# Taking turns between two streams of matmuls: a turn at every half group of products in place of every whole one

## The chip, the cores and the metric

The kernel runs on one core of one Trainium2 chip. The metric is the device time of one execution in microseconds (us). The engines are named as in the profile: PE is TensorE's matrix multiply and PEld its loading of weights, DVE is VectorE, ACT is ScalarE, POOL is GpSimd, SP is SyncE, which issues most of the DMAs. PSUM is the accumulator memory that PE writes; ACT and DVE copy ("evacuate") it to SBUF. Each engine works through its own instructions in one fixed order.

## The reference, cut to what matters

Forward and backward pass of two branches that share a normalised input: an S4 layer (a long convolution by FFT, with gradients for its parameters) and a gated feed-forward network. Sizes: 2048 rows, model width 576, hidden width 4608, 128 states. The result is the output and the gradients of the input and of eleven parameter arrays.

```python
def _A_ref(u, A_re, ..., Dskip):                       # S4
    K = jnp.einsum("dn,dnl,dn->dl", Cc, P, dB).real      # 576 kernels of length 2048
    Yf = rfft2(up) * rfft2(Kp)
    y = irfft2(Yf)[..., :L] + u * Dskip
def _B_ref(x, W_gate, W_up, W_down):                   # FFN
    gate = x @ W_gate; up = x @ W_up
    h = gate * (gate > 0) * up
    return h @ W_down
def f(...): xn = layernorm(A_u); return A_u + _A_ref(xn, ...) + _B_ref(xn, ...)
out, vjp = jax.vjp(f, ...); return out, *vjp(grad_out)
```

## The kernel before

Two Python generators write the program. `Ffn.gen` issues the feed-forward work, `S4.gen` the convolution work, and each hands control back with `yield us`, where `us` is its own figure for the work it has just issued. The loop at the end of the main function drives them: it takes one step of the FFN and adds its `us`; then it takes steps of S4 until S4's sum has caught up with `PACE` = 0.9 of the FFN's. S4 starts only when all four groups of the layer norm are done. So the places of the `yield`s in the FFN are the only places where S4's instructions can be issued, and the figures beside them say how much of S4 is issued there. Tile, the layer below, keeps this order as a priority when it puts each engine's instructions in a row: an instruction whose inputs it takes to be late can be passed by a later one.

The FFN runs over 12 chunks of 384 hidden columns (`FTC` = 3 blocks of 128) and 4 groups of 512 rows. For each chunk there are these pieces:

- `a_unit` (L228 on): three products of five matmuls (`NK` = 5, 128x512, L244): gate, up, and the gradient of h. Each has one PSUM bank of the pool `ps_mm`, which has three. When all three are issued, ACT makes `rg` (L252), DVE makes `upm` (L254), `hT` (L256), `dgT` (L262) and `duT` (L264), and one copy makes `dhb`. Before the `yield` of each product, `t_steps` (L273) issues four transposes per step into one of two `pt` banks, and a copy to `hN`, `dgN` or `duN`.
- `outdx` (L278 on): for one block of 128 rows, four products of 288 columns (L300): two of three matmuls for the output (`which` = 0) and two of six for the gradient of the input (`which` = 1). Each is copied to `osx`, and POOL issues a DMA that adds `osx` to `acc_dram` (L313).
- `dw_down` (L338): three groups of 16 matmuls of 144 columns in one bank. `dw_gu` (L354): two products of 16 matmuls of 384 columns. `dw_left` (L372): the same for the last 64 columns of width.

S4 works through PSUM banks of its own, `ps_s4`, of which there are three. `fwd1` (L627) transforms the long way; `mix` (L644) does the 16-point transform in two matmuls with 64 weight columns each, which write the upper and the lower half of one bank; `product` multiplies on DVE; `unmix` (L654) transforms back; `back2` (L684) ends it. `p2` makes the kernels and their gradients: long DVE and ACT steps (L838 to L876), then in `turn` and `sums` eight small matmuls (L901), eight transposes (L911) and eight matmuls (L925) a time, one bank each. Nearly every S4 bank is emptied by one copy (L68 on ACT or L62 on DVE, chosen by `Balance`, which keeps two running sums) and then used by a later S4 step.

For the last chunk the FFN yields the word "last" before the closing pieces: then all that is left of S4 is issued, and `Final` joins both branches (L1048 to L1093).

Of the kernel before, what the change touches and what calls it, by code (L numbers as in the profile page):

```python
# [21 lines left out]
ST = 16  # L22
DH = D // 2
NK = 5
DP = NK * P
Fc = 384
FTC = Fc // P
# [133 lines left out]
class Ffn:  # L161
# [68 lines left out]
    def a_unit(self, c, sg, ft, turns=()):  # L230

        g, nc = self.g, self.g.nc
        src = self.t_steps(turns)
        xT, gT = self.X[(c, sg)]
        fs = slice(ft * P, (ft + 1) * P)
        pss = []
        dhb = self.dh0.get(ft) if (c, sg) == (0, 0) else None
        for i, rhs in enumerate((xT, xT, gT)):
            if i == 2 and dhb is not None:
                continue  # L240
            w = self.wd[i]
            ps = g.psum_mm.tile([P, 512], F32, name="ps_mm")
            for k in range(NK):
                nc.tensor.matmul(ps[:], lhsT=w[:, k, fs], rhs=rhs[:, k, :], start=(k == 0), stop=(k == NK - 1))  # L244
            pss.append(ps)
            for _ in turns:
                next(src)
            yield NK * 0.2158 + len(turns) * 0.22
        ps_g, ps_u = pss[0:2]
        shp = [P, JS * P]  # L250
        rg = self.ep.tile(shp, BF16, name="rg")
        nc.scalar.activation(rg[:], ps_g[:], ACT.Relu)  # L252
        upm = self.ep.tile(shp, BF16, name="upm")
        nc.vector.scalar_tensor_tensor(upm[:], rg[:], 0.0, ps_u[:], op0=ALU.is_gt, op1=ALU.mult)  # L254
        hT = self.tp.tile(shp, BF16, name="hT")
        nc.vector.tensor_tensor(hT[:], rg[:], upm[:], op=ALU.mult)  # L256
        g.bal.add(d=1.6, a=0.48)
        if dhb is None:
            dhb = self.ep.tile(shp, BF16, name="dhb")[:]
            g.bal.copy(dhb, pss[2][:], 512)  # L260
        dgT = self.tp.tile(shp, BF16, name="dgT")
        nc.vector.tensor_tensor(dgT[:], dhb, upm[:], op=ALU.mult)  # L262
        duT = self.tp.tile(shp, BF16, name="duT")
        nc.vector.tensor_tensor(duT[:], dhb, rg[:], op=ALU.mult)  # L264
        self.T[(c, sg, ft)] = (hT, dgT, duT)
# [11 lines left out]
    def outdx(self, c, sg, j, last=None, turns=()):  # L277

        g, nc = self.g, self.g.nc
        t = sg * JS + j  # L280
        js = slice(j * P, (j + 1) * P)
        if last is None:
            o = self.op.tile([P, 2, D], BF16, name="osx")
        else:
            last.begin(t)
        src = self.t_steps(turns)
        Ts = [self.T[(c, sg, ft)] for ft in range(FTC)]
        for which in range(2):
            for hf in range(2):
                hs = slice(hf * DH, (hf + 1) * DH)  # L290
                if which == 0:
                    mms = [(Ts[ft][0], self.wf[:, 0, ft, hs]) for ft in range(FTC)]
                else:
                    mms = [(Ts[ft][1], self.wf[:, 1, ft, hs]) for ft in range(FTC)] + [(Ts[ft][2], self.wf[:, 2, ft, hs]) for ft in range(FTC)]
                mms = [(lt[:, js], rh) for lt, rh in mms]
                if last is not None:
                    mms = last.terms(t, which, hf) + mms
                ps = g.psum_mm.tile([P, 512], F32, name="ps_mm")
                for i, (lt, rh) in enumerate(mms):
                    nc.tensor.matmul(ps[:, :DH], lhsT=lt, rhs=rh, start=(i == 0), stop=(i == len(mms) - 1))  # L300
                if last is None:
                    g.bal.copy(o[:, which, hs], ps[:, :DH], DH)
                else:
                    last.take(t, which, hs, ps[:, :DH])
                next(src, None)
            if which == 0:
                yield FTC * 0.245
        if last is not None:
            last.end(t)
        elif c == 0:  # L310
            nc.gpsimd.dma_start(g.acc_dram[:, t, :, :], o[:])
        else:
            nc.gpsimd.dma_start(g.acc_dram[:, t, :, :], o[:], accum_op=ALU.add)  # L313
        yield FTC * 0.49

    def rows(self, c, i):

# [11 lines left out]
    def dw_down(self, c, q):  # L329
        g, nc = self.g, self.g.nc  # L330
        f0 = c * Fc
        gq = self.rows(c, q)
        if q % 2 == 0:
            self.obd = self.rp.tile([P, FTC, DH], BF16, name="obd")
        ps = g.psum_mm.tile([P, 512], F32, name="ps_mm")
        for ft in range(FTC):
            for st in range(ST):
                nc.tensor.matmul(ps[:, ft * 144:(ft + 1) * 144], lhsT=self.hN[:, st, ft * P:(ft + 1) * P], rhs=gq[:, st, :], start=(st == 0), stop=(st == ST - 1))  # L338
            if ft < FTC - 1:
                yield ST * 0.0625  # L340
        g.bal.copy(self.obd[:, :, (q % 2) * 144:(q % 2 + 1) * 144], ps[:, 0:FTC * 144].rearrange("p (f c) -> p f c", c=144), FTC * 144)
        if q % 2 == 1:
            hs = slice((q // 2) * DH, (q // 2 + 1) * DH)
            nc.sync.dma_start(self.dWd[f0:f0 + Fc, hs].rearrange("(t p) d -> p t d", p=P), self.obd[:])
        yield ST * 0.0625

    def dw_gu(self, c, k):
        g, nc = self.g, self.g.nc
        f0 = c * Fc
        xs = self.rows(c, 4 + k)  # L350
        for src, dst in ((self.dgN, self.dWg), (self.duN, self.dWu)):
            ps = g.psum_mm.tile([P, 512], F32, name="ps_mm")
            for st in range(ST):
                nc.tensor.matmul(ps[:, :Fc], lhsT=xs[:, st, 0:P], rhs=src[:, st, :], start=(st == 0), stop=(st == ST - 1))  # L354
                if st == ST // 2 - 1:
                    yield ST * 0.0813
            ob = self.rp.tile([P, Fc], BF16, name="obw")
            g.bal.copy(ob[:], ps[:, :Fc], Fc)
            nc.sync.dma_start(dst[k * P:(k + 1) * P, f0:f0 + Fc], ob[:])
            yield ST * 0.0813  # L360

    def dw_left(self, c):

# [870 lines left out]
```

## Time and profile before

| what | value |
| --- | --- |
| three runs, median (lowest to highest) | 1853.74 us (1851.06 to 1854.6) |
| the profiled execution, its own time | 1854.6 us |
| its span, first to last instruction | 1852.9 us |
| mean granted clock of TensorE | 0.989 |
| PE busy, instructions | 1744.4 us, 16257 |
| DVE busy, ACT busy | 1379.2 us, 1173.9 us |
| first and last S4 matmul start | 73.3 us, 1616.4 us |

How to read it: "busy" is the time in which an engine has an instruction under way, and matmuls overlap, so that a matmul of 288 columns that counts 288 ns follows the one before it after only 122 ns. An engine's "idle before" is named with what ended it. Lines such as L68 are those of a helper that many callers share; the tile that is written tells which caller it was. "issue" stands for idle time that no other instruction is seen to end.

### The profile page before, as it was taken

The page shows a single profiled execution, that of the slowest core. Times are in us where ns is not written, and L with a number is a line of the kernel's source. Part 1 is how long each engine was busy: PE and PEld are TensorE (multiplying, and loading weights), DVE is VectorE, ACT ScalarE, POOL GpSimd, SP SyncE. Part 2 cuts the span into 40 slices and gives each one's busy share as a digit, 9 for nine tenths or more (in the row PEclk, how much of TensorE's full clock was granted, in tenths as well). Part 3 has the DMA queues.
Part 4 walks back from the last instruction along what each step waited for, and adds up shares of the span by engine and source line. Part 5 has one row for each costly group of instructions (what it writes and reads, how often), then busy time and mean ns, then how long its engine had stood idle before and what let it go on. Part 6 is the DMA issues. An engine that isn't in the chain of part 4 may idle for free. (4 is left out here: it accounts for less than half of the span.)

```text
span 1852.9 us, 41883 instructions
## 1 busy us (share of the span) xinstructions
PE 1744.4 (94%) x16257; PEld 1182.4 (64%) x16257; DVE 1379.2 (74%) x3223; ACT 1173.9 (63%) x2647; POOL 206.5 (11%) x246
## 2 busy tenths in 40 slices
PE   7989989999999999999999999999999998899888
PEld 5655547667566666766766766766766764476556
DVE  7565875686798787787887889889878657924772
ACT  5865855686587488477487567657748746732432
POOL 0200002012012012002102101102201100010000
PEclk9989999999999999999999999999999999999999
DMA  8798988678567666776776856856754779785763
GB/s 287 264 323 292 328 237 261 195 182 220 182 129 192 191 184 166 211 187 139 207 202 136 233 156 154 236 159 122 195 174 97 183 240 269 203 216 179 232 195 102
DMA packets 236411, 373.26 MB, mean 201 GB/s; under 512 B 49202, under 2 KB 153140, under 8 KB 234676
## 3 DMA queue, kind: packets, MB, share of 16 engines
q1 hardware_dynamic: 210244, 304.08, 50.8%
q0 software_dynamic: 24384, 51.92, 18.8%
q10 hardware_dynamic: 1584, 14.60, 2.3%
q8 instruction: 127, 2.08, 0.4%
q14 instruction: 72, 0.59, 0.1%
HBM read 233.08 MB, written 137.43 MB: 200 GB/s over the span
## 5 line engine op out<-in xcount | busy, mean ns | idle before, releaser
L68 ACT CAST osx<-ps_mm 128x288 bf16<-128x288 f32 x684 | 261.7, 422 | 73.8 <-PE ps_mm L300 62.2
L313 POOL DMA_DIRECT2D acc_dram<-osx x160 | 139.8, 877 | 1038.1 <-ACT osx L68 581.0
L300 PE MATMUL ps_mm<-wf,dgT 128*128 128x288 bf16 x1152 | 209.1, 288 | 17.8 <-ACT osx L68 12.4
L354 PEld LDWEIGHTS <-rows 128*128 128x128 bf16 x1536 | 145.9, 98 | 95.9 <-issue 3.0
L300 PE MATMUL ps_mm<-wf,duT 128*128 128x288 bf16 x1152 | 207.1, 288 | 0.0
L300 PE MATMUL ps_mm<-wf,hT 128*128 128x288 bf16 x1152 | 186.4, 288 | 8.5 <-ACT osx L68 2.6
L244 PE MATMUL ps_mm<-xT,wd_158 128*128 128x512 bf16 x720 | 182.5, 379 | 0.7 <-ACT xT L153 0.7
L244 PE MATMUL ps_mm<-gT,wd_160 128*128 128x512 bf16 x705 | 181.4, 383 | 0.7 <-ACT obw L68 0.7
L244 PE MATMUL ps_mm<-xT,wd_159 128*128 128x512 bf16 x720 | 180.6, 379 | 0.0
L254 DVE SCALAR_TENSOR_TENSOR upm<-rg,ps_mm 128x512 bf16<-128x512 bf16 x144 | 98.3, 683 | 99.6 <-PE ps_mm L244 82.8
L338 PE MATMUL ps_mm<-rows,hN 128*128 128x144 bf16 x2304 | 158.2, 228 | 0.0
L338 PEld LDWEIGHTS <-hN 128*128 128x128 bf16 x2304 | 149.1, 99 | 8.1 <-issue 5.6
L300 PEld LDWEIGHTS <-dgT 128*128 128x128 bf16 x1152 | 109.7, 98 | 54.1 <-issue 25.8
L354 PE MATMUL ps_mm<-duN,rows 128*128 128x384 bf16 x768 | 138.6, 326 | 0.0
L354 PE MATMUL ps_mm<-dgN,rows 128*128 128x384 bf16 x768 | 136.6, 326 | 0.0
L300 PEld LDWEIGHTS <-hT 128*128 128x128 bf16 x1152 | 107.7, 98 | 42.7 <-issue 13.1
L300 PEld LDWEIGHTS <-duT 128*128 128x128 bf16 x1152 | 113.1, 98 | 32.0 <-issue 2.4
L68 ACT CAST obw<-ps_mm 128x384 bf16<-128x384 f32 x105 | 50.2, 478 | 125.8 <-PE ps_mm L354 89.6
L68 ACT CAST dhb<-ps_mm 128x512 bf16<-128x512 f32 x141 | 83.9, 595 | 66.3 <-PE ps_mm L244 64.6
L930 DVE TENSOR_REDUCE Sm<-pr 128x8 f32<-128x256 f32 x288 | 119.5, 415 | 3.6
L252 ACT ACTIVATE rg<-ps_mm 128x512 bf16<-128x512 f32 x144 | 86.9, 603 | 54.4 <-PE ps_mm L244 52.9
L244 PEld LDWEIGHTS <-wd_159 128*128 128x128 bf16 x720 | 65.4, 98 | 61.4 <-issue 1.2
(2513 smaller groups left out, 3516.2 us busy)
## 6 DMA issues: line engine op xcount, KB each, us to landing
acc_dram<-osx POOLq DMA_DIRECT2D x176, 288.0 KB, 4.8
gT<-in_gT_dram SPq DMA_DIRECT2D x48, 640.0 KB, 6.3
xT<-xT_dram SPq DMA_DIRECT2D x44, 640.0 KB, 6.2
rows<-in_gq_dram SPq DMA_DIRECT2D x48, 576.0 KB, 4.5
wf<-in_Wf_dram ACTq DMA_DIRECT2D x11, 1296.0 KB, 8.8
ex_dram<-exs SPq DMA_DIRECT2D x18, 640.0 KB, 5.6
ex<-ex_dram SPq DMA_DIRECT2D x36, 320.0 KB, 3.4
out_dram<-obw SPq DMA_DIRECT2D x96, 96.0 KB, 2.7
```

What stands on the lines that cost most here:

```text
L68: self.nc.scalar.copy(out, in_)
L244: nc.tensor.matmul(ps[:], lhsT=w[:, k, fs], rhs=rhs[:, k, :], start=(k == 0), stop=(k == NK - 1))
L252: nc.scalar.activation(rg[:], ps_g[:], ACT.Relu)
L254: nc.vector.scalar_tensor_tensor(upm[:], rg[:], 0.0, ps_u[:], op0=ALU.is_gt, op1=ALU.mult)
L300: nc.tensor.matmul(ps[:, :DH], lhsT=lt, rhs=rh, start=(i == 0), stop=(i == len(mms) - 1))
L313: nc.gpsimd.dma_start(g.acc_dram[:, t, :, :], o[:], accum_op=ALU.add)
L338: nc.tensor.matmul(ps[:, ft * 144:(ft + 1) * 144], lhsT=self.hN[:, st, ft * P:(ft + 1) * P], rhs=gq[:, st, :], start=(st == 0), stop=(st = ...
L354: nc.tensor.matmul(ps[:, :Fc], lhsT=xs[:, st, 0:P], rhs=src[:, st, :], start=(st == 0), stop=(st == ST - 1))
L930: nc.vector.tensor_reduce(out=Sm[:, vi, s0 + dd:s0 + dd + DG, :], in_=pr[:], op=ALU.add, axis=AX.X)
```

## The change

Five `yield`s of the FFN are split, so that control goes to S4 at about every half product; the figures are split with them, and their sum for a piece of work stays the same (in `outdx` 6 x 3 x 0.1225 instead of 3 x 0.245 + 3 x 0.49; with the closing terms of the last chunk two more are yielded). No instruction is added or taken away, and no buffer.

```diff
@@ a_unit: after two of the five matmuls, and after the product
             for k in range(NK):
                 nc.tensor.matmul(ps[:], lhsT=w[:, k, fs], rhs=rhs[:, k, :], ...)
+                if k == 1:
+                    yield 2 * 0.2158
             pss.append(ps)
             for _ in turns:
                 next(src)
-            yield NK * 0.2158 + len(turns) * 0.22
+            yield (NK - 2) * 0.2158 + len(turns) * 0.22
@@ outdx: at every three matmuls
                 for i, (lt, rh) in enumerate(mms):
                     nc.tensor.matmul(ps[:, :DH], lhsT=lt, rhs=rh, ...)
+                    if len(mms) - i == FTC + 1:
+                        yield FTC * 0.1225
                 if last is None:
                     g.bal.copy(o[:, which, hs], ps[:, :DH], DH)
...
-            if which == 0:
-                yield FTC * 0.245
+                if which + hf < 2:
+                    yield FTC * 0.1225
...
-        yield FTC * 0.49
+        yield FTC * 0.1225
@@ dw_down: at every 8 of 16 matmuls
                 nc.tensor.matmul(ps[:, ft * 144:(ft + 1) * 144], ...)
+                if st == ST // 2 - 1:
+                    yield ST * 0.03125
             if ft < FTC - 1:
-                yield ST * 0.0625
+                yield ST * 0.03125
...
-        yield ST * 0.0625
+        yield ST * 0.03125
@@ dw_gu: at every 4 of 16 matmuls
                 nc.tensor.matmul(ps[:, :Fc], lhsT=xs[:, st, 0:P], ...)
-                if st == ST // 2 - 1:
-                    yield ST * 0.0813
+                if st % 4 == 3 and st < ST - 1:
+                    yield 4 * 0.1625
             ob = self.rp.tile([P, Fc], BF16, name="obw")
             g.bal.copy(ob[:], ps[:, :Fc], Fc)
             nc.sync.dma_start(dst[k * P:(k + 1) * P, f0:f0 + Fc], ob[:])
-            yield ST * 0.0813
+            yield 4 * 0.1625
```

## The prediction

> **What bounds the kernel now.** First the page's busy times, then the stages, then PE's waits.
>
> ```profile
> span 1852.9 us, 41883 instructions
> ...
> PE 1744.4 (94%) x16257; PEld 1182.4 (64%) x16257; DVE 1379.2 (74%) x3223; ACT 1173.9 (63%) x2647; POOL 206.5 (11%) x246
> ```
>
> PE is the bound: 108.5 us of the span are all that it idles. The change adds no instruction, so it can only move that idle time, and the shorter delays that the overlap of matmuls hides in "busy". The stages (time, PE, PEld, DVE, ACT, POOL, clock, DMA share, GB/s) say where it lies:
>
> ```profile
> 0.00:73.00 73.00, 60.58 (x490) 41.05 (x491) 46.30 (x159) 46.24 (x99) 9.99 (x30) 1.00 0.86 285
> 73.00:295.00 222.00, 201.04 (x1488) 125.28 (x1486) 158.86 (x363) 151.00 (x336) 18.71 (x31) 0.94 0.88 285
> 295.00:902.00 607.00, 592.14 (x6070) 413.51 (x6067) 463.13 (x1015) 415.91 (x945) 87.84 (x91) 1.00 0.72 190
> 902.00:1502.00 600.00, 578.05 (x5800) 398.52 (x5798) 513.67 (x1175) 402.26 (x896) 76.08 (x78) 1.00 0.67 171
> 1502.00:1617.00 115.00, 98.99 (x658) 55.05 (x658) 83.10 (x264) 75.57 (x206) 6.92 (x8) 0.99 0.87 246
> ```
>
> Idle PE: 12.4 us before S4 starts at 73, then 21.0, 14.9, 22.0 and 16.0, and 22.4 after S4 has ended. Only the four stages with S4 in them, 73.8 us together, can answer to where S4's turns stand. In the last of them PE waits for the inverse transforms' writes (a copy into `fC` that waits for a DMA), and in the built order of the changed kernel all but one of the last 19 of its 32 `fC` tiles have as much PE work between their matmuls as before: I leave that stage out.
>
> Whom PE waits for, largest first:
>
> ```profile
> PE ps_mm L300 <- ACT osx L68: 15.0, 24, 2.4
> PE pt L273 <- DVE dgT L262: 11.5, 7, 4.0
> ...
> PE ps_s_2084 L627 <- ACT fA_2074 L68: 3.6, 1, 3.6
> PE pt L273 <- ACT hN L68: 3.3, 3, 2.9
> PE ps_mm L300 <- DVE osx L62: 2.9, 1, 2.9
> PE ps_s_1667 L627 <- DVE fA_1626 L62: 2.9, 1, 2.9
> ```
>
> Nothing large repeats; PE waits for copies out of banks, FFN's and S4's alike, a little at a time. So I also added up, over all starts of matmuls from 73 to 1617 us, the time by which each came later than the one before it allows when packed (122 ns after one of 288 columns, 216 after 512, 162 after 384, 62 after 144, 55 after 128, 25 after L901 and L925). This catches what "busy" hides. At the first matmul of a bank, with the price of a mode change (below) taken off, the delays come to 124 us: 69.4 at S4's banks, 34.1 at L300's, 15.8 at L273's, 4 at the rest.
>
> **The change, part by part.** Counted in the two built orders of PE, where a "turn" is S4 work between two FFN matmuls:
>
> *More and shorter turns.* S4's 1046 banks stand in 622 turns before and in 781 after; 424 are second or later in their turn before, 265 after (six in a row falls from four times to once). The delays before are 49.9 us at the 622 first ones (0.080 each) and 19.5 at the 424 later ones (0.046 each). A later one waits because the copy of a neighbour, 0.40 to 0.42 us on ACT for 288 columns, has not freed a bank. What moves out of a burst gets at least a quarter product in front of it: 0.37 us of L300, 0.43 of L244, 0.5 of L338, 0.65 of L354. I take it that these 159 lose their 0.046 us, **-7.3 us**, and that the delay at first ones, whose inputs come from DVE steps and DMAs at their own times, stays 49.9 in sum. Bounds: -19.5, if all later delays go, and +5.4, if each new first costs what the firsts cost (159 x (0.080 - 0.046)).
>
> *More mode changes.* `mix` uses 64 weight columns, and PE pays to go there and back:
>
> ```profile
> 181.23 0.60 PE L244 MATMUL ps_mm<-xT,wd_158 128*128 128x512 bf16 x2
> 181.77 0.31 PE L644 MATMUL ps_s_2640<-b_ug,FM 128*64 128x288 bf16 x2
> 182.01 0.82 PE L244 MATMUL ps_mm<-xT,wd_158 128*128 128x512 bf16 x3
> ```
>
> The second L244 starts at 181.459 (in the trace's rows), the pair follows 0.309 later where 0.216 is packed (0.093 lost), the next L244 after 0.246 where 0.122 is packed, and where another pair follows instead it starts after 0.147, so 0.1 is lost on leaving and 0.01 more in the spacing after it: 0.20 in all. Entries into `mix` from anything else are 143 before and 157 after: 14 x 0.20 = **+2.8 us**. Bounds: 0, where PE would have waited there anyway, and +2.8.
> The Trainium skill speaks against the change here: "TensorEngine Tiling (Array Packing)", Key Properties, says that a change of tiling mode drains TensorE. An estimate from "TensorE: Matmul & The Clock Gate", Single matmul latency, which gives about 166 ns beyond the streaming at full clock, would put two drains at 0.33 us and the 14 at +4.6, which would make the sum below -2.7; the row has less, and I use the row.
>
> *FFN banks.* A turn inside a product holds its `ps_mm` bank longer, and that product's copy is now issued behind the turn's copies. I measured in the orders how much PE work lies between the end of a product and the start of the one that takes its bank: for the 640 starts of L300 the mean stays, the starts with under 0.9 us in the commonest pairing rise from 36 to 51. By the trace a start with 0.6 to 0.8 us in between lost 0.083 us, one with 0.8 to 1 us 0.045, one with 1 to 1.2 us 0.100: no slope, so the price is **0**, with +1.5 (15 x 0.1) as the upper bound and -1.5 as the lower. The three banks of `a_unit` are freed only by L252 and L254 after the third product, before and after. The cover of L273's two `pt` banks changes as little (11 of 362 starts below 1.2 us, before and after).
>
> *What else moves with a turn.* S4's DMAs on SP (`A_ug`, `C_dk`, `ex`, `dkr`, `Kst`) and its long DVE and ACT steps are issued at most half a product (0.4 to 0.65 us) sooner or later, against 3 to 6 us to landing; SP passes no transfer over more than a turn, POOL's `acc_dram` adds keep their order, `Balance` moves seven copies between ACT and DVE (0.40 against 0.46 us). I price it at 0; the work that hides it is the FFN product under way. If that cover goes, what is late is `upm` (L254) behind a DVE step of 0.8 to 1.5 us, and then L244's banks: the wait is in the profile already, and a bound of +-4 us is one more or less of the longest DVE-made wait in the list above, 4.0.
>
> Sum: -7.3 + 2.8 + 0 + 0 = **-4.5 us** against the profiled execution's own 1854.6 (the span and 1.7 around it), hence 1850.1; that execution was 0.9 above the median of 1853.74, and against the median it is **1849.2**. Best bounds: -19.5 - 1.5 - 4 = -25; worst: +5.4 + 2.8 + 1.5 + 4 = +13.7.
>
> **The rivals.**
>
> *No change that can be told.* Within 0.2%, 3.7 us, one measurement of this kernel can't tell a change from none (three runs of one program lie 3.5 us apart). Priced by the cover of each S4 bank instead of its place in the turn, the delays go from 69.4 only to 67.5: covers under 0.6 us fall from 30 to 9, but those between 0.6 and 1 rise from 74 to 90. Then -1.9 + 2.8 = +0.9, **1854.6**. For it: Tile already puts S4 into products (50 of 99 turns within L244 products stand inside one). Against it: the delays of later ones in a turn are real rows.
>
> *A new wait at every new turn (slower).* PE runs in order; each of 159 new turns is one more place where it meets an S4 matmul whose input, made by DVE (`pr_z`, `pr`, `Y`; DVE is 86% busy from 902 to 1502), isn't there. At the firsts' 0.080: +5.4 + 2.8 = +8.2, **1862**. It decides from 0.052 us per new turn on (159 x 0.052 - 7.3 + 2.8 = 3.8). For it: 49.9 of the 69.4 us lie at firsts. Against: a later start also gives DVE more time.
>
> *The clock as well (much faster).* After the stall at 102 us PE ran at half speed:
>
> ```profile
> 102.00:107.00 5.00, 2.01 (x14) 1.06 (x13) 5.00 (x6) 4.54 (x6) 0.00 (x0) 0.90 0.96 337
> 107.00:112.00 5.00, 3.93 (x17) 1.85 (x17) 4.23 (x9) 3.77 (x9) 0.00 (x0) 0.50 1.01 392
> 112.00:118.00 6.00, 6.00 (x39) 4.41 (x38) 3.64 (x9) 2.41 (x7) 0.54 (x1) 0.65 0.98 322
> ```
>
> If the even turns of `fwd1` avoid that stall (2.9) and the slow clock after it (5 x 0.10 + 5 x 0.50 + 6 x 0.35 = 5.1), the sum is -4.5 - 2.9 - 5.1 = -12.5: **1841**. Against it: DVE is full there with three `exs` steps (L584), which stand together in the new order too.
>
> **How the numbers follow.** The forecast (faster, -4 to -8) has 0.34, the rival of the clock 0.08, no change 0.26, slower 0.32. So faster 0.42, same 0.26, slower 0.32; the predicted time is 1849.2. The range runs from 1838 to 1866: from the clock rival's time and 3 more down to the new waits' time and 4 more, inside the bounds on the good side (1829) and to just short of +13.7 (1867.4) on the other. The forecast's own range is 1845 to 1851.
>
> **What would show it.** Right: entries to L644 at 157 with the same 0.1 us lost on each side; fewer waits of L627, L654 and L911 on copies; idle PE from 73 to 1502 down from 57.8 by some 4; 1617 to the end unchanged at 236 us. The forecast is wrong if the idle time before S4's matmuls grows with the number of turns, or if L300's wait on `osx` (15.0) grows by more than 2 us. A half-speed stretch more or less (3.4 us of it cost 1.7) would blur all of this.

## The result, and the profile after

| | kernel before | changed kernel |
| --- | --- | --- |
| median (lowest to highest) of 4 runs each | 1854.17 us (1851.06 to 1855.16) | 1866.77 us (1864.97 to 1870.59) |
| profiled execution, its own time | 1854.6 us | 1865.62 us |

The ratio is 1.0074, with a 95% interval of 1.0053 to 1.0094: slower by 12.6 us, where -4.5 was forecast, and 0.8 us outside the range. These four runs of one kernel lie 4 to 6 us apart, so the sign is not in doubt; what it says of the change is another matter, to which the experiments come.

The page's busy times of the changed kernel:

```profile
span 1863.9 us, 41883 instructions
...
PE 1747.0 (94%) x16257; PEld 1180.6 (63%) x16257; DVE 1386.5 (74%) x3222; ACT 1176.7 (63%) x2648; POOL 206.9 (11%) x246
```

The same number of instructions, the same share of PE. DVE alone is busier by a sum that needs a reason, 7.3 us with one instruction less: its instructions have become longer. The stages, cut at the same events as before (start of S4, first L907, and so on; columns as before):

```profile
0.00:73.00 73.00, 60.07 (x491) 40.51 (x491) 46.30 (x159) 46.39 (x100) 9.99 (x30) 1.00 0.85 285
73.00:304.00 231.00, 205.03 (x1562) 128.44 (x1560) 160.47 (x362) 155.99 (x348) 27.49 (x38) 0.96 0.92 293
304.00:907.00 603.00, 586.84 (x5996) 406.25 (x5992) 466.69 (x1013) 411.41 (x933) 80.35 (x84) 1.00 0.69 183
907.00:1514.00 607.00, 578.82 (x5802) 399.18 (x5801) 515.92 (x1178) 403.87 (x897) 75.20 (x78) 0.99 0.66 170
1514.00:1628.00 114.00, 100.74 (x654) 55.80 (x653) 82.17 (x262) 75.45 (x204) 6.92 (x8) 0.97 0.88 246
```

Idle PE in the four stages with S4: 26.0, 16.2, 28.2 and 13.3 us, 83.6 together against 73.8 before. In the first three of them it is 70.4 instead of 57.8, where the prediction named some 4 us less as a sign of being right. What follows the last S4 matmul is unchanged (236.1 us against 236.5). The second stage has lengthened by 9 us and holds 74 matmuls more, the third is 4 shorter and holds 74 fewer; the fourth is 7 longer. By the ends of the FFN's chunks in the two traces, the changed kernel is 3 us ahead after the first chunk, 1 behind after the third and 13 behind after the eighth, and then stays at 11 to 13 (last matmul of `dw_gu` in each chunk). It is no single event, though it has one that stands out. The waits of PE, total us, times, longest:

```profile
PE ps_mm L302 <- ACT osx L68: 17.8, 17, 6.4
...
PE pt L275 <- DVE dgT L264: 9.1, 7, 3.6
PE ps_mm L302 <- DVE upm L256: 8.5, 10, 3.0
```

and of the kernel before, beside the 15.0 for `osx` that the prediction shows:

```profile
PE ps_mm L300 <- DVE upm L254: 2.0, 5, 0.8
```

(Lines have moved down: L300 is now L302, L273 L275, L254 L256, L252 L254, L627 L633, L644 L650, L313 L317, L354 L360, L828 and L829 L834 and L835.) The first line is the one that the prediction named as its test: fewer waits, but a larger sum, and one of 6.4 us. The waits for `upm` have grown by more, 6.5 us, 3.0 of it in one wait at 107 us, in a stall that PE has in both kernels. From 73 us to the last S4 matmul, waits of over 1 us number 31 and sum to 58.5 us; before, 26 and 48.2. These 10.3 us are nearly as much as the 11.0 by which the profiled executions differ.

The chain of that wait, in the timeline of the changed kernel (start, length, engine, line, operation; in brackets the idle time before it and what ended it):

```profile
285.14 1.20 POOL L834 COPY dkc<-dkr 128x512 bf16<-128x512 bf16 x1 [7.59 <-issue]
...
285.47 1.22 DVE L845 TENSOR_SCALAR W<-xa 128x640 f32<-128x640 f32 x1
...
286.32 1.73 POOL L835 TENSOR_TENSOR dkc<-dkr,lv 128x512 bf16<-128x512 bf16 x1
...
286.73 2.00 DVE L846 SCALAR_TENSOR_TENSOR W<-W,xa 128x640 f32<-128x640 f32 x1
...
288.00 1.64 POOL L834 COPY dkc<-dkr 128x512 bf16<-128x512 bf16 x1
...
288.76 0.74 ACT L847 ACTIVATE W<-W 128x640 f32<-128x640 f32 x1 [2.10 <-DVE W L846]
...
289.58 0.87 POOL L317 DMA_DIRECT2D acc_dram<-osx  x1
...
289.84 0.90 PE L302 MATMUL ps_mm<-wf,hT 128*128 128x288 bf16 x6 [1.81 <-ACT osx L68]
...
290.18 1.79 POOL L835 TENSOR_TENSOR dkc<-dkr,lv 128x512 bf16<-128x512 bf16 x1
...
291.61 2.09 POOL L317 DMA_DIRECT2D acc_dram<-osx  x2
...
297.94 0.40 ACT L68 CAST osx<-ps_mm 128x288 bf16<-128x288 f32 x1 [6.92 <-DMA acc_dram<-osx]
...
298.39 0.88 PE L302 MATMUL ps_mm<-wf,dgT 128*128 128x288 bf16 x3 [6.43 <-ACT osx L68]
...
300.71 0.86 POOL L317 DMA_DIRECT2D acc_dram<-osx  x1 [7.01 <-ACT osx L68]
```

Read it from the end. PE waits for a copy into `osx`; ACT waits to make that copy because all three `osx` buffers are still being added to `acc_dram`; these adds went out late, the first at 289.6 and two more from 291.6 on, because POOL issues them, and it had four instructions of S4 (`dkc`, 6.4 us of work) in its row before and between them. The wait of 1.81 us just before has another path: in ACT's row L847 stood ahead of the copy, and it waited 2.10 us for L846, a step of DVE that took 2.00 us while POOL worked on `dkc`. In the kernel before, the same stretch of POOL:

```profile
285.16 0.86 POOL L313 DMA_DIRECT2D acc_dram<-osx  x1 [2.74 <-ACT dk L68]
293.03 0.86 POOL L313 DMA_DIRECT2D acc_dram<-osx  x1 [7.01 <-ACT osx L68]
298.00 1.05 POOL L828 COPY dkc<-dkr 128x512 bf16<-128x512 bf16 x1 [4.10 <-DMA Sx<-s_dram]
299.01 1.49 POOL L829 TENSOR_TENSOR dkc<-dkr,lv 128x512 bf16<-128x512 bf16 x1
300.45 1.04 POOL L828 COPY dkc<-dkr 128x512 bf16<-128x512 bf16 x1
301.44 0.85 POOL L313 DMA_DIRECT2D acc_dram<-osx  x1
302.05 1.78 POOL L829 TENSOR_TENSOR dkc<-dkr,lv 128x512 bf16<-128x512 bf16 x1
303.48 2.09 POOL L313 DMA_DIRECT2D acc_dram<-osx  x2
```

Here too three adds stand behind and between the four `dkc` instructions. But they are the last three of their chunk: there are three `osx` buffers, and after these adds PE has `dw_down` and `dw_gu` to do, which need none. In the changed kernel the `dkc` instructions stand one add earlier, so that a fourth add, that at 300.7, comes behind the late three, and its copies had to wait for a buffer.

Two windows of the changed kernel (columns as in the stages) show what the wait brings behind it:

```profile
290.00:297.00 7.00, 1.63 (x12) 1.03 (x11) 0.00 (x0) 1.01 (x3) 3.71 (x4) 0.95 1.03 282
297.00:302.00 5.00, 3.61 (x25) 3.06 (x25) 0.00 (x0) 2.12 (x5) 0.86 (x1) 0.50 1.02 177
```

DVE has nothing to do in either; its next instruction, at 305.2, waits for PE. After the wait PE ran at half its clock.

The sum over the starts of matmuls (the delays that the prediction worked with), by where they lie:

| delays, us | before | after | change | forecast |
| --- | --- | --- | --- | --- |
| first S4 bank of a turn (622 turns, then 781) | 49.9 | 51.2 | +1.3 | 0 |
| later ones in a turn (424, then 265) | 19.5 | 16.6 | -2.9 | -7.3 |
| mode changes of `mix` (143, then 157 entries) | | | +2.8 (14 x 0.20) | +2.8 |
| first matmul of an `outdx` product (L300, L302) | 34.1 | 43.2 | +9.1 | 0 |
| of a `dw_gu` product (L354, L360) | 0.6 | 3.1 | +2.5 | 0 |
| of a group of transposes (L273, L275) | 15.8 | 12.4 | -3.4 | 0 |
| inside FFN products | 16.9 | 19.9 | +3.0 | 0 |

With 0.2 of small items these make +12.6; the two spans differ by 11.0. The line of the mode changes is the counted entries by the prediction's price. That price held: from an FFN matmul into `mix` the median start is 0.094 us late in both kernels, and 0.120 us out of it.

### The profile page after: what moved, and what is told of

The parts are those of the page before. It is cut to its first block, busy times and chain, and to the rows that moved or that the text cites. A ratio compares the mean times of both kernels' runs of the same rounds, so it can differ in the third digit from the quotient of the medians.

```text
span 1863.9 us, 41883 instructions
## 1 busy us (share of the span) xinstructions
PE 1747.0 (94%) x16257; PEld 1180.6 (63%) x16257; DVE 1386.5 (74%) x3222; ACT 1176.7 (63%) x2648; POOL 206.9 (11%) x246
## 5 line engine op out<-in xcount | busy, mean ns | idle before, releaser
L317 POOL DMA_DIRECT2D acc_dram<-osx x160 | 140.4, 881 | 1051.9 <-ACT osx L68 955.8
L302 PE MATMUL ps_mm<-wf,dgT 128*128 128x288 bf16 x1152 | 209.9, 288 | 25.1 <-ACT osx L68 15.4
L302 PE MATMUL ps_mm<-wf,duT 128*128 128x288 bf16 x1152 | 209.3, 289 | 0.0
L360 PEld LDWEIGHTS <-rows 128*128 128x128 bf16 x1536 | 144.9, 98 | 97.7 <-issue 8.6
L302 PE MATMUL ps_mm<-wf,hT 128*128 128x288 bf16 x1152 | 189.9, 288 | 10.3 <-DVE upm L256 4.9
L244 PE MATMUL ps_mm<-xT,wd_158 128*128 128x512 bf16 x720 | 186.0, 380 | 1.2 <-ACT xT L153 0.7
L244 PE MATMUL ps_mm<-xT,wd_159 128*128 128x512 bf16 x720 | 185.4, 379 | 0.0
L244 PE MATMUL ps_mm<-gT,wd_160 128*128 128x512 bf16 x705 | 185.3, 382 | 0.0
L256 DVE SCALAR_TENSOR_TENSOR upm<-rg,ps_mm 128x512 bf16<-128x512 bf16 x144 | 98.4, 683 | 86.8 <-PE ps_mm L244 62.6
L342 PE MATMUL ps_mm<-rows,hN 128*128 128x144 bf16 x2304 | 162.4, 229 | 0.3 <-ACT osx L68 0.3
L302 PEld LDWEIGHTS <-dgT 128*128 128x128 bf16 x1152 | 108.9, 98 | 60.8 <-issue 34.0
L360 PE MATMUL ps_mm<-dgN,rows 128*128 128x384 bf16 x768 | 141.0, 329 | 2.5 <-ACT rg L254 2.5
L360 PE MATMUL ps_mm<-duN,rows 128*128 128x384 bf16 x768 | 142.1, 326 | 0.0
L302 PEld LDWEIGHTS <-hT 128*128 128x128 bf16 x1152 | 107.7, 98 | 45.0 <-issue 14.4
L302 PEld LDWEIGHTS <-duT 128*128 128x128 bf16 x1152 | 110.4, 99 | 32.4 <-issue 3.4
L254 ACT ACTIVATE rg<-ps_mm 128x512 bf16<-128x512 f32 x144 | 86.8, 603 | 56.4 <-PE ps_mm L244 54.1
L244 PEld LDWEIGHTS <-wd_158 128*128 128x128 bf16 x720 | 66.2, 98 | 56.2 <-issue 5.2
```

## The experiments

All ratios are against the kernel before, run in the same batch on the same chip (medians 1852.77, 1851.36, 1853.55, 1853.96 and 1853.4 us in the five batches), with 95% intervals.

### Which part of the change loses the time

Four kernels with one part each. First `outdx` alone, as in the change; then `outdx` with turns at the ends of products only, so that no turn holds a bank open; then `a_unit` alone; then `dw_down` and `dw_gu` alone. The first, third and fourth take the change's own hunks. The second:

```diff
-            if which == 0:
-                yield FTC * 0.245
+                if which + hf < 2:
+                    yield (1 + which) * FTC * 0.1225
...
-        yield FTC * 0.49
+        yield FTC * 0.245
```

> Only outdx takes turns at every three matmuls (L300); all else as before. 702 turns instead of 622, 122 of them inside an L300 product instead of 40, 153 mode changes instead of 143. Theory banks (a turn inside an open product holds its ps_mm bank, and the product's copy goes behind the turn's copies): this part carries most of the loss, +6 to +12 us, with delays at L300's bank starts up from 34 to 42 or more. Theory turns (each new turn costs alike, 0.08 us): 80 of the 159 new turns, half of the loss, +4 to +8. Theory luck (the new order merely meets other single long waits): anything from -8 to +12.

> Only outdx is changed: a turn at the end of each of its four products, after the copy is issued, none inside a product. 684 turns, 58 inside L300 products. Theory banks: no loss, -3 to +2 us, delays at L300's bank starts at 34 or less. Theory turns: 62 new turns, +3 to +6. Theory luck: anything from -8 to +12.

> Only a_unit takes a turn after two of its five matmuls. 676 turns, 133 inside an L244 product instead of 50. Theory banks: the three banks of a_unit are freed only after the third product in both versions, so -2 to +3 us. Theory turns: 54 new turns, +3 to +6. Theory luck: anything from -8 to +12.

> Only dw_down and dw_gu take turns at every half group. 643 turns, 96 inside an L354 product instead of 62. Theory banks: these products are long (1.0 and 2.6 us), a bank is held long in either case, -2 to +3 us. Theory turns: 21 new turns, 0 to +3. Theory luck: anything from -8 to +12.

| kernel | median, us | ratio | turns | L300's delays, us (34.1 before) |
| --- | --- | --- | --- | --- |
| `outdx` as in the change | 1864.16 | 1.0056 (1.0037 to 1.0075) | 702 | 34.7 |
| `outdx`, ends of products only | 1869.64 | 1.0087 (1.0057 to 1.0116) | 684 | 36.3 |
| `a_unit` | 1864.78 | 1.0057 (1.0035 to 1.0079) | 676 | 46.1 |
| `dw_down`, `dw_gu` | 1856.89 | 1.0021 (1.0005 to 1.0037) | 643 | about 33 |

That open banks are the loss falls with the second kernel: turns at ends only are no better, and L300's delays hardly rise in either of the first two. In the third they rise by 12, though `a_unit` has no turn inside L300's products at all. And two parts that touch different places each lose about as much as the whole: the first, third and fourth row, which together are the change, lose 11.4, 12.0 and 4.1 us, 27.5 where the change loses 12.6. Parts of one mechanism should have added up. The theory of the turns, with at most 8 us for any part, missed the first three, and the second row, with 16.9 us by its median, lies above every range that was expected for it. This pointed to another theory: every edit redraws the order in which Tile places some thousand instructions, and the kernel before is a lucky draw.

### Is the order before a lucky draw?

`PACE` says how much of S4 is issued per unit of FFN work. Changing it by 0.2% or 0.5%, in both kernels, redraws the order and leaves the length of turns alone.

```diff
-PACE = 0.9
+PACE = 0.895     # and 0.898, 0.902, 0.905
```

> The kernel before with PACE 0.895 instead of 0.9: the same places for turns, the same amount of S4 at them to 0.6%, another order in detail (601 turns, 138 mode changes). Theory luck (the order of before is a good draw among many, and any other order costs more): +4 to +14 us. Theory turns (finer turns as such cost): -2 to +3, since turns are no more than before.

> The kernel before with PACE 0.905: 630 turns, 144 mode changes. Theory luck: +4 to +14 us. Theory turns: -2 to +3.

> The changed kernel with PACE 0.895: 766 turns, 141 mode changes. Theory luck: anywhere between 0 and +20 us against the kernel before, and apart from the changed kernel's +13 by 4 or more in either this or the next run. Theory turns: +11 to +14, like the changed kernel.

> The changed kernel with PACE 0.905: 803 turns, 156 mode changes. Theory luck: anywhere between 0 and +20 us, as for the run at 0.895. Theory turns: +12 to +15.

> The kernel before with PACE 0.898, 0.2% less S4 at each turn: 612 turns, 142 mode changes, yet only 956 of the 2186 stretches of like matmuls in its order stand as before (the changed kernel keeps 1188). Theory draw (the time is that of a few long waits, and every new order draws them anew, whatever it was changed for): anywhere between -4 and +15 us against the kernel before. Theory turns (the change's loss comes from its shorter turns): -2 to +2.

> The kernel before with PACE 0.902: 616 turns, 145 mode changes. Theory draw: anywhere between -4 and +15 us; the five orders of the kernel before (0.895 to 0.905) then spread over 10 us or more. Theory turns: -2 to +2.

> The changed kernel with PACE 0.898: 772 turns, 148 mode changes. Theory draw: anywhere between -4 and +17 us, and the mean of the changed kernel's five orders within 5 us of the mean of the five of the kernel before. Theory turns: +10 to +14.

> The changed kernel with PACE 0.902: 770 turns, 157 mode changes. Theory draw: anywhere between -4 and +17 us. Theory turns: +10 to +14.

| PACE | kernel before, ratio | changed kernel, ratio |
| --- | --- | --- |
| 0.895 | 1.0044 (1.0029 to 1.0060) | 0.9991 (0.9976 to 1.0007) |
| 0.898 | 1.0003 (0.9984 to 1.0021) | 1.0017 (1.0000 to 1.0034) |
| 0.9 | 1 | 1.0074 (1.0053 to 1.0094) |
| 0.902 | 1.0106 (1.0076 to 1.0136) | 1.0028 (1.0010 to 1.0046) |
| 0.905 | 1.0080 (1.0061 to 1.0097) | 1.0076 (1.0055 to 1.0097) |
| mean | 1.0047 | 1.0037 |

The kernel before spreads over 1.06% of its time, 20 us, between 0.9 and 0.902, more than the change moves it. Its own value is the best of its five; the changed kernel's, with 1.0074, is not told apart from the last of its five, and at 0.895 it is no slower than the kernel before at its best. The difference of the means is -0.0009, and from the scatter of each five (0.0047 and 0.0037) its standard error is 0.0027: whether shorter turns as such gain or cost anything is not told apart, down to about half a per cent. The changed kernel was slower as it stood, and that is all the comparison of one order with one order could say. A step of `PACE` also shifts S4 against the FFN a little, so the ten are not pure draws: both columns are higher on average above 0.9 (1.0093 and 1.0052) than below it (1.0024 and 1.0004), and part of the spread may be that. Taken pair by pair, at the same `PACE`, the changed kernel stands between 0.0078 better and 0.0074 worse, with the same mean and standard error.

What a poor draw is made of can be seen: from the first S4 matmul to the last, waits of over 1 us sum to 44.6 us in the fastest of these eight and to 64.8 and 67.5 in the two orders at 0.905. But the kernel before at 0.902 has 56.4 and is slowest of all, so the long waits are not the whole of it.

One place in POOL's row, the one shown above, can be followed through all fourteen orders (the two kernels, the four with parts and these eight). The first `dkc` instruction stands behind either 28 or 29 of the DMAs into `acc_dram`:

| DMAs ahead of the first `dkc` | orders | ratios (mean) | PE's waits for `osx` from 280 to 310 us |
| --- | --- | --- | --- |
| 29 | the kernel before; `dw_down` and `dw_gu` alone; both kernels at 0.895 and 0.898 | 0.9991 to 1.0044 (1.0013) | 0.2 to 2.0 us |
| 28 | the changed kernel; both `outdx` kernels and `a_unit` alone; both kernels at 0.902 and 0.905 | 1.0028 to 1.0106 (1.0070) | 3.3 to 8.8 us |

This would be why the parts don't add up, and why both columns are higher above 0.9: one and the same step of the row is taken or not. With the place the same, the changed kernel is not the slower one (mean 1.0004 against 1.0016 of the kernel before with 29, 1.0059 against 1.0093 with 28), though so few orders settle nothing. It is a count made afterwards, and orders with 28 can differ elsewhere too; the next runs take `dkc` out of this place.

### Is it POOL?

Of the waits of the changed kernel the 6.4 us one has a chain that can be cut: put the first four `dkc` instructions on DVE and leave PE's and SP's orders exactly as they are. `v` is DVE.

```diff
-            nc.gpsimd.tensor_copy(dkc[:, :, 0, :], dkv)
-            nc.gpsimd.tensor_tensor(dkc[:, :, 1, :], dkv, ...)
+            (v if hf == 0 and gi < 2 else nc.gpsimd).tensor_copy(dkc[:, :, 0, :], dkv)
+            (v if hf == 0 and gi < 2 else nc.gpsimd).tensor_tensor(dkc[:, :, 1, :], dkv, ...)
```

Done in the changed kernel, in the kernel before, which lacks the wait, and in the changed kernel at `PACE` 0.905, where PE waits 6.6 us for `osx` behind the same `dkc` instructions, at 300.9 us. A fourth kernel is the changed one with all 36 `dkc` instructions on DVE.

> The changed kernel with the dkc steps of the first two groups of p2 (L834, L835; four instructions) on DVE instead of POOL. The orders of PE and SP stay as in the changed kernel, ACT's and DVE's differ in a few rows. Theory POOL (the largest new wait of the changed kernel, 6.4 us at 298, comes from acc_dram adds that stand behind two dkc steps on POOL, so that osx buffers are late): that wait and the half-speed stretch behind it go, -6 to -9 us against the changed kernel, so +4 to +7 against the kernel before; the rest of the loss stays spread over smaller waits. Rival (osx is late by the adds' own time to landing): no change, +11 to +14.

> The kernel before with the same four instructions on DVE; PE's, ACT's and SP's orders are unchanged. Theory POOL: its adds don't stand behind dkc steps there, so -2 to +2 us. Rival (dkc on POOL or DVE matters by itself): -5 or less.

> The changed kernel at PACE 0.905 (14 us over the kernel before, with a wait of 6.8 us at 301) with the same four instructions on DVE; PE's and SP's orders unchanged. Theory POOL: -6 to -9 us, so +5 to +8 against the kernel before. Rival: +12 to +16.

> The changed kernel with all 36 dkc instructions on DVE; PE's order differs in 1715 of some 64000 lines. Theory POOL: a further -2 to -4 us against the run with the first two groups alone, from the waits of 0.6 to 2.1 us for acc_dram later on, less what 32 more instructions on DVE cost. Theory draw: the order is partly drawn anew, so -8 to +8 against that run.

| kernel | median, us | ratio | the same without the edit |
| --- | --- | --- | --- |
| changed, four on DVE | 1857.23 | 1.0028 (1.0008 to 1.0049) | 1.0074 (1.0053 to 1.0094) |
| before, four on DVE | 1852.23 | 0.9995 (0.9979 to 1.0011) | 1 |
| changed at 0.905, four on DVE | 1861.9 | 1.0050 (1.0034 to 1.0066) | 1.0076 (1.0055 to 1.0097) |
| changed, all on DVE | 1843.73 | 0.9950 (0.9931 to 0.9969) | 1.0074 (1.0053 to 1.0094) |

With four instructions moved, the changed kernel gives back 8.5 us of its loss (0.0046 of 1854, with some 5 us either way by the two intervals), and the kernel before, with the same edit, nothing. It isn't that its adds had been free, as was expected: the edit brings the three that stood behind `dkc` forward from 301.4, 303.5 and 304.1 us to 295.3, 298.0 and 300.1, and nobody had waited for them. In the third row it is 4.8, less than expected and not clear of the noise: that order has other waits of L302 on `osx`, 20.0 us of them after the edit and 23.2 before it. POOL of the first kernel, in the stretch shown above:

```profile
284.35 0.84 POOL L317 DMA_DIRECT2D acc_dram<-osx  x1 [6.88 <-ACT osx L68]
286.46 0.86 POOL L317 DMA_DIRECT2D acc_dram<-osx  x1 [1.27 <-ACT osx L68]
288.67 0.85 POOL L317 DMA_DIRECT2D acc_dram<-osx  x1 [1.35 <-ACT osx L68]
294.78 0.86 POOL L317 DMA_DIRECT2D acc_dram<-osx  x1 [5.26 <-ACT osx L68]
```

Now POOL waits for ACT, not ACT for POOL: each add goes out when its `osx` is made. The first is that of 289.58 in the changed kernel, 5.2 us sooner; it landed at 290.3 instead of 297.8. DVE is no quicker with its step for ACT here (L847 waits 3.01 us for L846, 2.10 in the changed kernel), so what went is the wait for the adds. In the list of waits of this kernel ACT's wait for the adds falls from 19.1 us to 11.0, and PE's for `osx` from 17.8 to 12.2, its longest from 6.4 to 3.0:

```profile
PE ps_mm L302 <- ACT osx L68: 12.2, 15, 3.0
...
ACT osx L68 <- DMA acc_dram<-osx: 11.0, 7, 3.7
```

And DVE's own steps in that stretch are short again, beside the two `dkc` instructions that it has taken over:

```profile
285.05 0.60 DVE L834 COPY dkc<-dkr 128x512 bf16<-128x512 bf16 x1 [1.66 <-DMA dkr<-dk_dram]
285.56 1.02 DVE L835 TENSOR_TENSOR dkc<-dkr,lv 128x512 bf16<-128x512 bf16 x1
...
289.99 0.49 DVE L845 TENSOR_SCALAR W<-xa 128x640 f32<-128x640 f32 x1
290.52 0.82 DVE L846 SCALAR_TENSOR_TENSOR W<-W,xa 128x640 f32<-128x640 f32 x1
```

0.49 and 0.82 us, where the changed kernel took 1.22 and 2.00 while POOL worked on `dkc`.

### All of it on DVE, in three orders

The same edit in the kernel before and in the best of the changed orders:

```diff
-            nc.gpsimd.tensor_copy(dkc[:, :, 0, :], dkv)
-            nc.gpsimd.tensor_tensor(dkc[:, :, 1, :], dkv, ...)
+            v.tensor_copy(dkc[:, :, 0, :], dkv)
+            v.tensor_tensor(dkc[:, :, 1, :], dkv, ...)
```

> The kernel before with all 36 dkc instructions on DVE. Theory POOL (the adds behind dkc steps cost in every order): -5 to -10 us against the kernel before, like the changed kernel with this edit against that with four instructions moved. Theory draw: between -8 and +12, by the order alone, since the same edit for the first four instructions moved this kernel by 0.

> The changed kernel at PACE 0.895 with all dkc instructions on DVE. Theory POOL: -5 to -10 us against that kernel without the edit (0.999 of the kernel before), so -7 to -12 against the kernel before. Theory draw: between -10 and +10.

The kernel before took 1848.24 us, 0.9971 (0.9957 to 0.9985), at the near end of what was expected; the changed kernel at 0.895 took 1852.58, 0.9993 (0.9977 to 1.0009), and there the edit brings nothing (0.9991 without it), against the theory. In the changed kernel at 0.9 it brought more than either theory allowed, 13.5 us against the run with four instructions moved. So the changed kernel with all `dkc` on DVE, 1843.73, is the fastest kernel of the study, faster than the one before by 10 us in its batch and faster than the changed one by 23; how much of this is the edit and how much the order that came with it, three orders with gains of 0.0124, 0.0029 and nothing don't settle. Its page:

```profile
span 1845.8 us, 41856 instructions
...
PE 1743.0 (94%) x16257; PEld 1178.7 (64%) x16257; DVE 1382.2 (75%) x3258; ACT 1177.2 (64%) x2648; POOL 156.5 (8%) x210
```

DVE has 36 instructions more than in the changed kernel and is busy 4.3 us less.

## Why the prediction was wrong, point by point

- **More and shorter turns, -7.3.** Half right. The assumption about the first banks of a turn held: 159 more of them, and their delays sum to 51.2 us in place of 49.9. The rival of a new wait at every turn, which asked for 0.052 us per new turn, is excluded for this order: it got 0.008 (1.3 / 159). But the later ones lost 2.9 us and not 7.3: those that remain wait longer (0.063 us each, 0.046 before), as they would if it was the cheap ones that left the bursts. Taking the mean for those that move was the mis-sizing. That this rival had named the sign, slower, is luck. The no-change rival, which priced S4's banks by their cover (69.4 to 67.5), had them right: 67.8.
- **More mode changes, +2.8.** Right: entries went to 157, as counted in the order, and each lost what it had lost before.
- **The end, unchanged.** Right: 236.1 us after the last S4 matmul.
- **The clock rival.** At 102 to 118 us the changed kernel did run faster than before (0.66 and 1.00 in the second and third window, where 0.50 and 0.65 were):

```profile
102.00:107.00 5.00, 2.04 (x17) 1.22 (x15) 5.00 (x6) 4.75 (x7) 0.00 (x0) 1.00 0.95 298
107.00:112.00 5.00, 4.63 (x30) 3.21 (x30) 3.76 (x9) 3.12 (x9) 0.00 (x0) 0.66 1.00 394
112.00:118.00 6.00, 5.95 (x49) 4.59 (x47) 5.89 (x11) 5.41 (x14) 1.08 (x2) 1.00 0.95 369
```

  The stall itself stayed (PE 2.04 us busy of 5), and other stalls, that at 297 among them, cost the same clock: between the first and the last S4 matmul, 34.1 us at half speed in both executions. The rival was right to look there and wrong that it would not be given back.
- **FFN banks, 0, bounds 1.5 either way.** Wrong by size: L300's starts alone went from 34.1 to 43.2 us. The working looked for the loss in how long a turn holds a bank open; that is not where it is, since turns at ends of products only lose as much (1.0087). The starts became late because `osx` did, and `upm` (waits of 17.8 and 8.5 us instead of 15.0 and 2.0).
- **What else moves, 0, bounds 4 either way.** This is the step that failed. It said that POOL's adds keep their order and so cost nothing. They keep it among themselves; but POOL has one row for the adds and for `dkc`, and the new order put the first two `dkc` pairs one add earlier, so that a block of `outdx` was still to come that needed a buffer from the adds behind them. Costing a move at nothing would have needed POOL's row compared, as PE's was. PE waited 6.4 us for `osx`, and taking the four instructions out of POOL's row gave back 8.5 us, that wait and what came with it. The forecast's own test ("if L300's wait on `osx`, 15.0, grows by more than 2 us") was met, at 17.8. `upm`, which the working named as the next to be late, was late as well, by more than the 4 us of the bound and at L302 rather than at L244; that stayed with the four instructions moved (8.4). The 4.0 us that gave the bound is a wait at 1764 us, after S4 has ended, where no turn stands.
- **The rest, 3 to 5 us** (1857.23 against 1853.96 by the medians, 1.0028 by the ratio), lies in waits of up to 4 us that stand elsewhere than before. It is a balance: by the ends of the chunks in the profiled executions, against the kernel before, the edit turned a loss of 5.1 us in the second chunk into a gain of 1.1, but the third to eighth lose 12.5 us with it (10.8 without), and the remaining ones gain 7.9. No run ties these waits to the length of turns. The nine other orders of the `PACE` runs speak for chance, though they don't show it: only one of them was faster than the kernel before by the medians, and its interval holds 1. The prediction summed mechanisms on top of the order before as if that were a mean one. Its bounds were each worked out from one term at a time; the scatter of orders, 0.0047 of the time or 9 us for the kernel before, is larger than every term in the sum. That a range of 1838 to 1866 nearly held the time is owed to the bounds that stood in for it.

Left open: whether shorter turns gain or lose anything below half a per cent; which of the small waits make up the loss of the third to eighth chunk; and how much of the gain of `dkc` on DVE would stay in other orders. A fourth `osx` buffer, the other way to cut the chain, was not tried: there is no room for it in SBUF.

## What to carry to other kernels

Where a scheduler places the instructions, measure the scatter first: shift a harmless constant by a fraction of a per cent in both kernels, and compare the means of several orders; one order against one order tells only which draw was better. Then look for what the bad orders share: here it was one step in the row of one engine. When a change moves work in time, compare the row of every engine that issues something the critical path needs, the little used ones above all: an 11% busy POOL held PE for 6.4 us, because a DMA that frees a buffer stood behind work that nobody was in a hurry for. Standing behind it is not yet a cost, as the kernel before shows: ask who needs the buffer next. A bank that is late says whom to ask next; follow it to the first engine that was busy with something else.

## What the hardware showed unexpectedly

Small steps on POOL lengthen DVE's. The `dkc` groups, in the kernel before:

```profile
L829 POOL TENSOR_TENSOR dkc<-dkr,lv 128x512 bf16<-128x512 bf16 x18 | 30.1, 1670 | 0.0
...
L828 POOL COPY dkc<-dkr 128x512 bf16<-128x512 bf16 x18 | 21.0, 1164 | 246.5 <-issue 242.3 <-DMA Sx<-s_dram 4.1
```

and in the kernel before with all of them on DVE (sum, then mean in ns):

```profile
L829 DVE TENSOR_TENSOR dkc<-dkr,lv 128x512 bf16<-128x512 bf16 x18 | 18.3, 1018 | 0.0
...
L828 DVE COPY dkc<-dkr 128x512 bf16<-128x512 bf16 x18 | 10.6, 588 | 3.5 <-DMA dkr<-dk_dram 3.5
```

DVE took on 28.9 us of work, and its busy time went from 1379.2 to 1379.5 us: about as much had been lost in DVE's other instructions while POOL had these 51.1 us of its own. Summed directly, the DVE instructions that overlap with `dkc` on POOL in the kernel before took 20 us longer than others of their forms; the rest is not accounted for, and between the two kernels, with the same work, DVE's busy time differs by 7.3 us anyway. In the rows at 285 to 289 us of the changed kernel the two DVE steps end 0.35 and 0.68 us after the POOL instruction that they overlap, with 0.49 and 0.82 us of work of their own: they look like steps that could do little until POOL's was over.

The Trainium skill has the rule: "SBUF — State Buffer", Who interferes with whom, says that DVE and GpSimd share one pair of ports to SBUF under an exclusive lock, and that a DVE instruction with two SBUF inputs contends with a GpSimd instruction that reads SBUF. L846 has two inputs in SBUF, and agrees: 0.82 us became 2.00. L845 has one, and took 1.22 us instead of 0.49, of which the rule for two inputs says nothing. The page lets the instruction that is issued second wait until the first has finished; the 36 instructions that cost DVE nothing to take over agree with that in sum, though no run here isolates one pair.

Clock: after each of the two stalls of the changed kernel shown here (at 102 and at 291 to 298 us) PE ran at half speed for 3 to 5 us (0.50 granted from 297 to 302, and 0.66 from 107 to 112, where 0.50 for 3.4 us comes to the same). By an estimate from the window from 297 to 302 this is about 1.8 us (half of PE's 3.61 busy) on top of the wait. In the kernel before the first of the two was followed by some 10 us at half speed (0.90, 0.50 and 0.65 granted in the three windows that the prediction shows).
